# LayerNorm steps of Wo's second wave and of w1 set to new places in a hand-written order

## The chip, the cores and the metric

The kernel runs on one core of a Trainium2 chip. The metric is the device time of one execution in microseconds (us). The engines are TensorE (PE, matmuls), VectorE (DVE), ScalarE (ACT), GpSimd (POOL) and SyncE (SP, which here only issues DMAs). Each engine works through its own queue in the order in which the program issues to it, and waits where an instruction needs a result of another engine or a DMA.

## The reference

An adaptive-LayerNorm block with two parts. `mod = silu(c) @ w_mod` gives six rows `sa, ca, ga, sb, cb, gb`. Then, for x of 2048 tokens by 1024:

```
h = layernorm(x) * (1 + ca) + sa
x = x + ga * A(h)        # segment-recurrent attention, 32 heads; its last product is o @ Wo
h = layernorm(x) * (1 + cb) + sb
x = x + gb * B(h)        # B: gelu(layernorm(h) @ w1), shifted by 1 or 2 tokens in four
                         # column groups, @ w2, + h; then gelu(layernorm(.) @ w3) @ w4, + .
```

What matters here is the way from `o @ Wo` to `@ w1`. For each token: the product is multiplied by `ga`, x is added, a LayerNorm gives `u`, which is modulated by `(1 + cb)` and `sb`, and a second LayerNorm gives `z`. `z`, transposed, is an operand of `@ w1`. Both the sum (`x1`) and the modulated `u` are needed later, so both are written to HBM.

## The kernel before, in words

Tokens are in 16 tiles of 128. Tile 0 holds the first 32 tokens and the last 96; tile t holds tokens 32 + 128(t - 1) and the 127 after it. The part that the change touches is a stretch of 144 units of TensorE, numbered n = 0 to 143, of 8 matmuls of 128x512 each.

Units 0 to 111 are `o @ Wo` in two waves of 56 (`wave(0)`, `wave(1)`, L938 to L1005). A wave covers 1024 tokens (8 tiles) by all 1024 columns, as a 2x2 block product with seven products in place of eight (Strassen's form, Winograd's variant). The products come in the order 1, 2, 5, 6, 3, 7, 4 (`ORDER`), each in two halves of four units. So in wave 1 product 1 is units 56 to 63, 2 is 64 to 71, 5 is 72 to 79, 6 is 80 to 87, 3 is 88 to 95, 7 is 96 to 103 and 4 is 104 to 111. Four PSUM banks ("b") serve products 1, 6, 7 and 4, four others ("d") products 2, and then 5 and 3. Behind a product's second half (`after`, L956) either ScalarE copies a bank (`snap`, L946), or VectorE forms a result: `fin` (L949) adds a copy to the bank (L952) where there is one and multiplies by `ga` (L954). Tiles 8 to 11 get their two column halves after products 2 and 3, tiles 12 to 15 after 7 and 4. VectorE also forms the sums and differences of the operand: `sums` (L992, the operation is L1002) has four for each half, which `sums1[hf][k]` numbers: k = 0 is X (for product 5), 1 is f21 (product 7), 2 is f11 (product 6), 3 is f12 (product 3).

Units 112 to 143 are `@ w1` (`A_units`, L1225): four blocks of 512 tokens, eight units each, with a gelu on ScalarE behind each unit (L1231). They go round eight banks, so unit n needs the gelu of unit n - 8. Block 0 needs tiles 0 to 4 of z transposed, block 1 tiles 4 to 8, block 2 tiles 8 to 12, block 3 tiles 12 to 15 and the rest of tile 0.

Between, each tile t goes through these steps:

- `load_x2` (L1114): x from HBM, a DMA issued by POOL, into one of two buffers.
- `C1_x` (L1138): POOL adds x to the two column halves (L1141), and they are written to HBM (L1145; issued by POOL up to tile 8, by SP from tile 9).
- `ln_stats` (L1122): VectorE takes statistics (two BN_STATS, an aggregation and two small ones, L1125 to L1129), POOL the power and one product (L1131, L1132).
- `C1_u` (L1147): ScalarE normalizes into u (two instructions, L1151), one of three buffers.
- `C1_mod` (L1153): VectorE multiplies and adds two rows (L1155, L1156) and takes statistics of the result (L1125 again), POOL the power and one product.
- `C1_z` (L1160): ScalarE normalizes into z (L1163).
- `C1_out` (L1165): a transposing DMA of z (L1174) and the write of u (L1168), issued by ACT up to tile 8 and by SP from tile 9.

The order is written by hand. `put(n, ...)` hangs functions behind unit n, and in a `manual_schedule` the units are issued with what hangs behind them, so every queue's order follows from the numbers:

```
for n in range(8, 144):
    units[n]()
    for f in at.get(n, []):
        f()
```

Each tile had a start (L1255), and its steps followed it at fixed distances: x at 0, statistics at 2, u at 3, modulation at 6, z at 8, out at 9. Also hung in this stretch: `load_w1` (unit 79), `late_slots` (98: the rest of tile 0's transposes and one write, on ACT's queue), `open_h1` and `load_w2` (111). Loads of w3 that follow the stretch ("ring", L1303) are placed by the scheduler and stand between the last tiles' DMAs on SP's queue.

Of the kernel before, what the change touches and what calls it, by code (L numbers as in the profile page):

```python
# [29 lines left out]
NTT = S // P  # L30
# [30 lines left out]
def kernel(ctx, tc, A_x, A_mem0, A_Wq, A_Wk, A_Wv, A_Wo, A_seg_len, B_x, B_w1, B_w2, B_w3, B_w4, c, w_mod, out,  # L61
# [102 lines left out]
    def p_rows(t):  # L164

        if t == 0:
            return [(slice(0, 32), slice(0, 32)), (slice(32, 128), slice(S - 96, S))]
        return [(slice(0, P), slice(32 + P * (t - 1), 32 + P * t))]

    def first_pass(late_hook):  # L170
# [15 lines left out]
        ves = mpool.tile([P, NTT], F32, name="ves")  # L186
# [748 lines left out]
        x1s = {}  # L935
# [178 lines left out]
        def load_x2(t):  # L1114
            if t < NTT and t not in xts2:
                xts2[t] = tp.tile([P, D], BF16, name="xt2")
                for rows, toks in p_rows(t):
                    nc.gpsimd.dma_start(xts2[t][rows, :], x2[toks, :])
# [3 lines left out]
        def ln_stats(t, halves, rstd):  # L1122
            stt = bsm.tile([P, 2, 6], F32, name="ln_st")
            for i in range(2):
                nc.vector.bn_stats(out=stt[:, i, :], in_=halves[i])  # L1125
            mv = bsm.tile([P, 2], F32, name="ln_mv")
            nc.vector.bn_aggr(out=mv[:], in_=stt[:])
            nc.vector.tensor_scalar(mv[:, 1:2], mv[:, 1:2], EPS, None, ALU.add)
            nc.vector.tensor_scalar(mv[:, 0:1], mv[:, 0:1], -1.0, None, ALU.mult)  # L1129
            nmr = bsm.tile([P, 1], F32, name="ln_nmr")  # L1130
            nc.gpsimd.tensor_tensor(rstd, mv[:, 1:2], mhalf[:], ALU.pow)  # L1131
            nc.gpsimd.tensor_tensor(nmr[:], mv[:, 0:1], rstd, ALU.mult)  # L1132
            ln[t] = nmr[:], rstd

        def halves_of(ap):
            return [ap[:, n * 512:(n + 1) * 512] for n in range(2)]

        def C1_x(t):  # L1138
            for n in range(2):
                cs = slice(n * 512, (n + 1) * 512)  # L1140
                nc.gpsimd.tensor_tensor(x1s[t, n][:], x1s[t, n][:], xts2[t][:, cs], ALU.add)  # L1141
            for n in range(2):
                cs = slice(n * 512, (n + 1) * 512)
                for rows, toks in p_rows(t):
                    (nc.sync if t > 8 else nc.gpsimd).dma_start(x1_d[toks, cs], x1s[t, n][rows, :])  # L1145

        def C1_u(t):  # L1147
            nmr, rstd = ln[t]
            us[t] = tu.tile([P, D], BF16, name="u")
            for n, dst in enumerate(halves_of(us[t][:])):  # L1150
                nc.scalar.activation(dst, x1s[t, n][:], ACT.Identity, bias=nmr, scale=rstd)  # L1151

        def C1_mod(t):  # L1153
            u = us[t]
            nc.vector.tensor_tensor(u[:], u[:], cb1_b[:], ALU.mult)  # L1155
            nc.vector.tensor_tensor(u[:], u[:], sb_b[:], ALU.add)  # L1156
            rstd = bsm.tile([P, 1], F32, name="ln_rstd")
            ln_stats(t, halves_of(u[:]), rstd[:])

        def C1_z(t):  # L1160
            nmr, rstd = ln[t]
            zs[t] = (tz if t else tz0).tile([P, D], BF16, name="z")
            nc.scalar.activation(zs[t][:], us[t][:], ACT.Identity, bias=nmr, scale=rstd)  # L1163

        def C1_out(t):  # L1165
            C1b(t)()
            for rows, toks in p_rows(t):
                (nc.sync if t > 8 else nc.scalar).dma_start(u_d[toks, :], us[t][rows, :])  # L1168
# [7 lines left out]
        def C1b(t):  # L1176
            def f():
                if t == 0:
                    turn_z(t, slice(0, 32), 0)
                elif t == 8:  # L1180
                    for r in (slice(0, 64), slice(64, 96), slice(96, P)):
                        turn_z(t, r, 32 + P * (t - 1) + r.start)
                else:
                    turn_z(t, slice(0, P), 32 + P * (t - 1))
            return f

        def next_a(key, hf=None):
            def f():
                for x in range(2) if hf is None else (hf,):
                    load_a(1, key, x)  # L1190
            return f
# [7 lines left out]
        U1, sums1, _ = wave(1)  # L1199
# [39 lines left out]
        def put(n, *fs):  # L1239
            at.setdefault(n, []).extend(fs)  # L1240
# [6 lines left out]
        put(31, next_a((0, 0)))  # L1247
        put(39, next_a((1, 0)))
        put(47, next_a((1, 1)))
        for n, (hf, k) in {57: (0, 0), 59: (1, 0), 72: (0, 1), 74: (0, 2), 76: (1, 1), 78: (1, 2), 83: (0, 3), 85: (1, 3)}.items():  # L1250
            put(n, sums1[hf][k])
        put(79, load_w1)
        put(98, late_slots)
        put(111, open_h1, load_w2)
        starts = [40, 45, 50, 55, 60, 76, 81, 86, 97, 101, 105, 109, 113, 116, 119, 122]  # L1255
        for t, n in enumerate(starts):
            put(max(n - 9, starts[t - 2] if t > 1 else 0), lambda t=t: load_x2(t))
            put(n, lambda t=t: C1_x(t))
            put(n + 2, lambda t=t: ln_stats(t, [x1s[t, k][:] for k in range(2)], ves[:, t:t + 1]))
            put(n + 3, lambda t=t: C1_u(t))  # L1260
            put(n + 6, lambda t=t: C1_mod(t))
            put(n + 8, lambda t=t: C1_z(t))
            put(n + 9, lambda t=t: C1_out(t))
        put(134, check_b)
        for k in range(KT):
            put(135 + k, lambda k=k: check_a(k))
# [977 lines left out]

    cond_box = []
    first_pass(None if no_fallback else (lambda: cond_box.append(load_flag())))
    if no_fallback:
        return
# [51 lines left out]
```

## Time and profile before

| | us |
|---|---|
| median of 5 runs | 1460.7 |
| lowest, highest | 1455.13, 1481.52 |
| the profiled execution | 1456.59 |
| its span | 1454.8 |
| TensorE busy | 1399.4 (96%) |
| VectorE busy | 980.2 (67%) |
| ScalarE busy | 688.2 (47%) |
| POOL busy | 474.5 (33%) |
| matmuls of `o @ Wo` (L987) | 776.1 to 977.3 |
| matmuls of `@ w1` (L1230) | 977.3 to 1045.1 |

In lines of the timeline the columns are start, length, engine, line, operation, output<-inputs, shapes and count; in square brackets stands how long the engine sat idle before it and what ended that. Consecutive instructions of one kind are merged into one line with their count. In windows, "PEclk" is the share of full speed that TensorE's clock was granted.

### The profile page before, as it was taken

The numbers are of one execution on the slowest core, as the hardware profiler recorded it, in microseconds if no ns is written. First come the engines' busy times: TensorE is split into PE (matmuls) and PEld (weight loads), VectorE is DVE, ScalarE is ACT, GpSimd is POOL, SyncE is SP. The second block draws the span as 40 slices with busy tenths as digits, with TensorE's granted clock in tenths as the row PEclk, the third lists the DMA queues.
The fourth block names the chain that finished last, engine by engine and source line by source line (L and its number), as shares of the span: only waits on it lengthen the run. The fifth ranks groups of instructions, "written<-read, shape, count | busy, mean of one in ns | idle before, by whom it ended". The sixth has DMA issues, their size and how long they took to land.

```text
span 1454.8 us, 24753 instructions
## 1 busy us (share of the span) xinstructions
PE 1399.4 (96%) x9126; PEld 739.6 (51%) x9126; DVE 980.2 (67%) x1995; ACT 688.2 (47%) x1468; POOL 474.5 (33%) x656
## 2 busy tenths in 40 slices
PE   6998999999999999999999999999899999999998
PEld 4675555555555555555555444444343444444443
DVE  6627776777776777777754647887257567666684
ACT  3625556565665656566664013226355650056400
POOL 6120321503222202220001025655224663645525
PEclk9999999999999999999999999999999999999999
DMA  9778978878787776777759999968499783477812
GB/s 327 272 237 201 184 169 201 213 177 205 178 198 195 171 177 172 177 198 181 160 137 305 362 372 296 303 198 255 134 289 244 234 277 107 152 235 250 282 40 79
DMA packets 389237, 310.69 MB, mean 214 GB/s; under 512 B 199658, under 2 KB 336874, under 8 KB 385266
## 3 DMA queue, kind: packets, MB, share of 16 engines
q1 hardware_dynamic: 356576, 244.03, 62.0%
q0 software_dynamic: 13856, 46.16, 9.2%
q10 hardware_dynamic: 18674, 18.83, 4.6%
q8 instruction: 73, 1.20, 0.3%
q14 instruction: 58, 0.48, 0.1%
HBM read 199.38 MB, written 59.02 MB: 178 GB/s over the span
## 4 chain that ended last, share of the span: by engine, by line
PE 73%; DVE 10%; DMA 9%; ACT 3%; issue 3%; POOL 1%; SPq 0%; DVEq 0%; POOLq 0%; ACTq 0%
PE acc L649 26%; PE acc L987 10%; PE bank_b L1509 7%; PE bank_b L1458 6%; PE acc L323 3%; PE bank_d L1458 3%; DMA s<-OTw_d 3%; PE bank_e L1509 2%; PE bank_d L1509 2%; PE acc L333 2%; PE acc L1230 2%; PE acc L1368 2%; PE ps_o L774 2%; PE bank_e L1458 2%; DMA wk<-in_A_Wk_dram 2%
## 5 line engine op out<-in xcount | busy, mean ns | idle before, releaser
L649 PEld LDWEIGHTS <-T 128*128 128x128 f16 x1408 | 129.9, 97 | 122.2 <-issue 6.8
L617 ACT COPY snap<-acc 128x480 f32<-128x480 f32 x264 | 146.0, 565 | 90.8 <-PE acc L649 84.1
L987 PE MATMUL acc<-wstream,s 128*128 128x512 f16 (+1 forms) x864 | 187.3, 379 | 1.2 <-DMA wstream<-in_A_Wo_dram 0.7
L649 PE MATMUL acc<-hs,T 128*128 128x480 f16 x704 | 159.7, 366 | 4.1 <-DVE QT L621 2.0
L649 PE MATMUL acc<-hh,T 128*128 128x480 bf16 (+1 forms) x704 | 162.5, 366 | 0.4 <-DVE KT L621 0.3
L987 PEld LDWEIGHTS <-s 128*128 128x128 f16 (+1 forms) x864 | 84.2, 98 | 103.8 <-DVE s L1002 1.8
L1458 PEld LDWEIGHTS <-ring 128*128 128x128 f16 (+1 forms) x784 | 76.7, 98 | 101.1 <-issue 9.4
L799 POOL DMA_DIRECT2D OTw_d<-OT x32 | 24.8, 774 | 259.7 <-DMA OT<-O 208.7
L761 ACT ACTIVATE E<-ps_s 99x495 bf16<-99x495 f32 (+2 forms) x160 | 88.0, 551 | 40.5 <-PE ps_s L757 40.0
L649 PE MATMUL acc<-hh,wq 128*128 128x480 bf16 x464 | 105.6, 366 | 0.0
L781 DVE TENSOR_TENSOR O<-ps_o,rin_all 99x384 bf16<-99x384 f32 (+1 forms) x192 | 97.3, 510 | 3.9
L1423 ACT COPY snap<-bank_b 128x512 f32<-128x512 f32 x72 | 41.8, 586 | 105.4 <-PE bank_b L1509 58.2
L621 DVE TENSOR_TENSOR KT<-acc,snap 128x480 bf16<-128x480 f32 x116 | 74.4, 654 | 22.5 <-PE acc L649 16.0
L774 PE MATMUL ps_o<-V,E 99*128 99x129 bf16 (+1 forms) x704 | 81.0, 220 | 8.5 <-DVE O L781 2.9
L1509 PEld LDWEIGHTS <-hq 128*128 128x128 bf16 (+1 forms) x560 | 54.7, 98 | 66.2
L763 DVE TENSOR_TENSOR E<-E,maskB 99x495 bf16<-99x495 bf16 (+1 forms) x128 | 53.4, 418 | 47.9 <-ACT E L761 46.2
L1292 DVE TENSOR_TENSOR ring<-ring 128x1024 f16<-128x1024 bf16 (+1 forms) x64 | 78.4, 1244 | 4.3 <-PE bank_b L1509 3.8
L774 PEld LDWEIGHTS <-E 99*128 99x128 bf16 (+1 forms) x704 | 57.0, 98 | 46.0 <-DVE O L781 4.8
L779 ACT ACTIVATE O<-ps_o,rin_all 99x128 bf16<-99x128 f32 x192 | 56.7, 370 | 41.7 <-DVE rin_all L776 41.4
L1509 PE MATMUL bank_b<-ring,hq 128*128 128x512 f16 (+1 forms) x336 | 73.2, 379 | 0.0
L1462 ACT ACTIVATE hq<-join 128x512 bf16<-128x512 f32 x84 | 52.8, 630 | 42.9 <-DVE join L1466 42.9
L621 DVE TENSOR_TENSOR VT<-acc,snap 128x480 bf16<-128x480 f32 x90 | 58.0, 651 | 21.5 <-PE acc L649 15.3
(268 smaller groups left out, 2681.4 us busy)
## 6 DMA issues: line engine op xcount, KB each, us to landing
OTw_d<-OT POOLq DMA_DIRECT2D x32, 512.0 KB, 5.9
wstream<-WoT_d SPq DMA_DIRECT2D x16, 1024.0 KB, 8.8
wstream<-in_B_w_dram SPq DMA_DIRECT2D x28, 512.0 KB, 5.2
ring<-in_B_w_dram SPq DMA_DIRECT2D x28, 512.0 KB, 5.5
ring<-in_B_w_dram SPq DMA_DIRECT2D x8, 1792.0 KB, 10.1
s<-OTw_d SPq DMA_DIRECT2D x13, 1024.0 KB, 8.1
wstream<-in_A_Wo_dram SPq DMA_DIRECT2D x11, 1024.0 KB, 11.5
wq<-in_A_Wq_dram SPq DMA_DIRECT2D x16, 512.0 KB, 5.7
```

What stands on the lines that cost most here:

```text
L617: nc.scalar.copy(t[:], st[q][bank][:, 0:CH])
L621: nc.vector.tensor_tensor(view(d, i), chunks(st[q][bank]), chunks(st[q][s_]), ALU.add)
L649: nc.tensor.matmul(acc[:, 0:CH], lhsT=B[:, k, :], rhs=A[:, k, :], start=(j in (1, 2, 5) and k == 0), stop=(k == 3), skip_group_check=True)
L761: nc.scalar.activation(E[:rows, 0:o], ps[:rows, 0:o], ACT.Exp, scale=DH ** -0.5)
L763: nc.vector.tensor_tensor(E[:rows, 0:o], E[:rows, 0:o], mk[:rows, 0:o], ALU.mult)
L774: nc.tensor.matmul(ps[:, i, :], lhsT=state["e", h, t // 5][:k, c:c + P], rhs=V[:k, t, 0:DH + 1], start=True, stop=True)
L779: nc.scalar.mul(O[:rows, t, :], ps[:rows, i, 0:DH], rin[:, i:i + 1])
L781: nc.vector.tensor_tensor(O[:rows, ts[0]:ts[0] + n, :], ps[:rows, 0:n, 0:DH], rin[:, :, None].to_broadcast([rows, n, DH]), ALU.mult)
L987: nc.tensor.matmul(acc[:], lhsT=A[:, k, i * P:(i + 1) * P], rhs=B[:, k, :], start=(j in (1, 2, 5) and hf == 0 and k == 0), stop=(hf == 1 a ...
L1292: return nc.vector.tensor_tensor(dst, a, b, op)
L1458: nc.tensor.matmul(acc[:], lhsT=B[:, k, q * P:(q + 1) * P], rhs=A[:, k, :], start=(start and k == 0), stop=(k == 3), skip_group_check=True)
L1509: nc.tensor.matmul(acc[:], lhsT=L3[:, k, i * P:(i + 1) * P], rhs=R3[:, k, :], start=(start and k == 0), stop=(k == 13), skip_group_check=True)
```

## The change

The table of starts with fixed distances gives way to two tables, one for the statistics and one for the modulation. x stands two units ahead of the statistics, u one behind them; z follows the modulation by two units (three from tile 8 on), out by three (four). Where several steps hang behind one unit they are sorted: x, load, statistics, u, modulation, z, out. Before they stood in the order of the tiles.

Six of the eight operand sums of wave 1 move as well: f21 from units 72 and 76 to 65 and 66, f11 from 74 and 78 to 72 and 73, f12 from 83 and 85 to 76 and 79.

In units, before and after:

| tile | 3 | 4 | 5 | 6 | 7 | 8 | 9 | 10 | 11 | 12 | 13 | 14 | 15 |
|---|---|---|---|---|---|---|---|---|---|---|---|---|---|
| statistics before | 57 | 62 | 78 | 83 | 88 | 99 | 103 | 107 | 111 | 115 | 118 | 121 | 124 |
| statistics after | 57 | 61 | 63 | 74 | 79 | 95 | 98 | 101 | 104 | 112 | 114 | 117 | 119 |
| modulation before | 61 | 66 | 82 | 87 | 92 | 103 | 107 | 111 | 115 | 119 | 122 | 125 | 128 |
| modulation after | 61 | 66 | 77 | 81 | 85 | 98 | 104 | 107 | 110 | 114 | 117 | 119 | 122 |

Tiles 0 to 2 keep these two places. On SP's queue the scheduler's ring loads move too: four of six stood around the last two tiles' transposes (two ahead of tile 14's, two ahead of tile 15's) and now stand behind them all; two others now stand ahead of tile 13's.

```diff
-        for n, (hf, k) in {57: (0, 0), 59: (1, 0), 72: (0, 1), 74: (0, 2), 76: (1, 1), 78: (1, 2), 83: (0, 3), 85: (1, 3)}.items():
+        for n, (hf, k) in {57: (0, 0), 59: (1, 0), 65: (0, 1), 66: (1, 1), 72: (0, 2), 73: (1, 2), 76: (0, 3), 79: (1, 3)}.items():
             put(n, sums1[hf][k])
...
-        starts = [40, 45, 50, 55, 60, 76, 81, 86, 97, 101, 105, 109, 113, 116, 119, 122]
-        for t, n in enumerate(starts):
-            put(max(n - 9, starts[t - 2] if t > 1 else 0), lambda t=t: load_x2(t))
-            put(n, lambda t=t: C1_x(t))
-            put(n + 2, lambda t=t: ln_stats(t, [x1s[t, k][:] for k in range(2)], ves[:, t:t + 1]))
-            put(n + 3, lambda t=t: C1_u(t))
-            put(n + 6, lambda t=t: C1_mod(t))
-            put(n + 8, lambda t=t: C1_z(t))
-            put(n + 9, lambda t=t: C1_out(t))
+        stat = [42, 47, 52, 57, 61, 63, 74, 79, 95, 98, 101, 104, 112, 114, 117, 119]
+        mod = [46, 51, 56, 61, 66, 77, 81, 85, 98, 104, 107, 110, 114, 117, 119, 122]
+        steps = []
+        for t in range(NTT):
+            late = t > 7
+            xn = stat[t] - 2
+            steps += [(max(xn - 9, stat[t - 2] - 2 if t > 1 else 0), 1.5, lambda t=t: load_x2(t)),
+                      (xn, 1, lambda t=t: C1_x(t)),
+                      (stat[t], 2, lambda t=t: ln_stats(t, [x1s[t, k][:] for k in range(2)], ves[:, t:t + 1])),
+                      (stat[t] + 1, 3, lambda t=t: C1_u(t)),
+                      (mod[t], 4, lambda t=t: C1_mod(t)),
+                      (mod[t] + 2 + late, 5, lambda t=t: C1_z(t)),
+                      (mod[t] + 3 + late, 6, lambda t=t: C1_out(t))]
+        for n, _, f in sorted(steps, key=lambda x: x[:2]):
+            put(n, f)
```

## The prediction

> **What bounds the kernel now.** I read the page's busy table first, then TensorE's waits and its timeline around the changed stage, then the other engines' timelines there.
>
> ```profile
> PE 1399.4 (96%) x9126; PEld 739.6 (51%) x9126; DVE 980.2 (67%) x1995; ACT 688.2 (47%) x1468; POOL 474.5 (33%) x656
> ```
>
> TensorE is the bound: only 1454.8 - 1399.4 = 55.4 us of the span are idle on it. A schedule edit can gain only what it waits for in this stage. Its waits from 880 to 1045 us (columns: total, times, longest):
>
> ```profile
> PE acc L1230 <- DMA s<-z: 5.4, 1, 5.4
> PE acc L1230 <- ACT u L1151: 3.0, 1, 3.0
> ```
>
> No wait in Wo's second wave, two in w1. TensorE's timeline shows where:
>
> ```profile
> 977.28 27.79 PE L1230 MATMUL acc<-zA,s 128*128 128x512 bf16 x128
> 1008.07 15.66 PE L1230 MATMUL acc<-s,s 128*128 128x512 bf16 x64 [3.00 <-ACT u L1151]
> 1029.16 16.02 PE L1230 MATMUL acc<-s,s 128*128 128x512 bf16 x64 [5.43 <-DMA s<-z]
> ```
>
> 128 matmuls of w1 take 27.79 us, so 64 should take 13.9. The two later blocks took 15.66 and 16.02, which is 1.8 and 2.1 us more. The windows of L1230 show why (length, PE busy, PEld busy, granted clock, DMA share, GB/s):
>
> ```profile
> 1009.00:1013.00 4.00, 4.00 (x13) 1.41 (x12) 0.57 0.38 133
> 1029.00:1033.00 4.00, 3.84 (x10) 1.36 (x11) 0.50 0.05 13
> 1037.00:1041.00 4.00, 4.00 (x20) 1.85 (x19) 1.00 0.00 0
> ```
>
> After each idle stretch the clock is half for about 3.5 us. The two waits therefore cost 3.0 + 5.4 + 1.8 + 2.1 = 12.3 us. That is the most that can be gained here (0.84%).
>
> Next VectorE and POOL ahead of unit 72 (units are numbered as in the schedule; one is 8 matmuls, 1.73 us; unit 111 ends at 977.28, so unit 72 starts at 908.1). VectorE:
>
> ```profile
> 891.24 2.28 DVE L1002 TENSOR_TENSOR s<-s,s 128x4096 f16<-128x4096 bf16 x1
> 895.78 1.19 DVE L1155 TENSOR_TENSOR u<-u,cb_b 128x1024 bf16<-128x1024 bf16 x1 [2.26 <-ACT u L1151]
> ...
> 903.62 0.69 DVE L1155 TENSOR_TENSOR u<-u,cb_b 128x1024 bf16<-128x1024 bf16 x1 [2.42 <-ACT u L1151]
> ...
> 906.76 0.68 DVE L952 TENSOR_TENSOR snap<-acc,snap 128x512 f32<-128x512 f32 x1
> ```
>
> The last line reads the bank that unit 72 writes again (product 5 takes the four accumulator banks of product 2). It ends at 907.45, 0.6 us before it is due.
>
> POOL, and VectorE beside it (two views):
>
> ```profile
> 894.15 2.27 POOL L1141 TENSOR_TENSOR x<-x,xt 128x512 f32<-128x512 f32 x2
> 896.37 1.14 POOL L1145 DMA_DIRECT2D x_d<-x x2
> ...
> 952.21 2.27 POOL L1141 TENSOR_TENSOR x<-x,xt 128x512 f32<-128x512 f32 x2
> ```
> ```profile
> 952.25 2.79 DVE L954 TENSOR_TENSOR x<-snap,ga_b 128x512 f32<-128x512 f32 x1
> ```
>
> The multiplication with two operands in SBUF, 0.69 us elsewhere, took 2.79: it ended 0.56 us after POOL's pair of additions. Where VectorE comes second it waits for the whole pair.
>
> **What the Trainium skill says.** "SBUF — State Buffer", section "SBUF: two separate sides", has the port pair of VectorE and GpSimd as an exclusive lock for the whole instruction, for VectorE operations with two SBUF inputs too; the 2.79 us agrees. "TensorE: Matmul & The Clock Gate", Part 1, halves the clock after an idle window of about 3.4 us and restores it after as much work; here 3.0 us of idling were enough, so the trace decides. The same page ("Architectural detail") calls ScalarE's and VectorE's queues strict FIFO, on which the arguments on order rest; every stretch of the timelines shows it.
>
> **The change part by part.** Write S(t) for a tile's statistics (1.7 us on VectorE), M(t) for its modulation with second statistics (3.15 us free of POOL, 3.65 when it starts inside an addition), fin for a product's result (1.35 with a snapshot, 0.65 without), x(t) for POOL's addition of x (2.27).
>
> *Nothing is added or removed*: the same instructions move. What counts is the order in each queue.
>
> *Units 57 to 71.* Between the second sum (ends 893.5) and the first fin at 906.76 VectorE now does M3, S4, M4 with 2.26 and 2.42 us of waiting. After, it does S4, M3, S5, two sums (moved from units 72 and 76 to 65 and 66), M4, fin. S4 needs x(4), which ends at 896.42 as before, so S4 ends at 897.6. M3 takes 3.65: 901.25. S5: 902.95. Two sums of 2.28: 907.5. M4: 910.65. The L952: 911.35. Unit 72 waits from 908.1 to 911.4: 3.3 us. But x(5) is moved directly behind x(4) and its write, so it starts at 897.5, in a tie with M3. The pair holds VectorE off until 899.8, which makes M3 about 1.6 longer: wait 4.9. I take the middle, 4.1, and 1.8 for the clock (the 3.0 us wait cost that): **5.9 us lost**; ends 3.3 (clock kept) and 6.9. The u of M4 doesn't decide: S4's power stands behind x(5) and its write on POOL (900.95), u(4) ends near 903.3, M4 starts at 907.5.
>
> *Units 92 to 111* (times without that delay, which shifts TensorE and what depends on it alike). From the last fin of product 3 (950.9) VectorE does S8 1.7; S9, which ends 4.15 later because x(9) stands behind S8's power on POOL (0.8 + 2.27 + 1.1); M8 3.65; four fins 5.6; S10 and S11 3.4; two waits for the pairs x(10), x(11), about 1.6 each; M9 and M10 6.6; three fins 2.0. Sum: 981.3. The fins of product 7 come after S10 now, so unit 106 may wait about 0.7.
>
> *Last tiles.* M11 waits 1.1 for x(12)'s pair and ends near 986; one fin, S12 and S13: 990.8. S12's power stands behind x(13) and an xt load on POOL (991.2), u(12) takes 1.5, M12 ends at E = 995.9. Behind its power POOL does x(14) and x(15) together: E + 5.3. M13 waits for that pair: E + 8.3. S15: E + 10.1. Its power (up to 1 us, against M14) and u(15): E + 12.6. Now ScalarE, in order: z(13) stands behind u(15), and the gelu of unit 121 behind z(13): E + 14.5 = 1010.4. Unit 129 takes that gelu's bank and is due at 977.28 + 17 x 1.737 = 1006.8: **a wait of about 3.6 us**. Tile 12's transpose, behind the writes of x(14) and x(15) on SP, is issued at E + 6.7 = 1002.6; transposes of this stage land after 2.4 to 8.4 us, so block 2 (due 1005.1) waits up to 6 in the same place, not on top. With the clock 5.4, plus the 0.7: **6.1 us lost** in place of 12.3. Tile 15's transpose is issued near 1016 and the ring loads that stood before the last two transposes on SP now stand after them (one but for tile 13); with 4 to 6.5 us it lands by 1022.5, before block 3 is due (1005.1 + 5.4 + 13.9 = 1024.4). Cover there: 2 us.
>
> *Other moves cost nothing.* u ahead of the previous z on ScalarE in wave 1 (z is used some 90 units later), f11 and f12 earlier (f11 ready about 918 and 921, due at 922 and 929; f12 about 925 and 930, due at 936 and 943; units 83 to 85 get that time back), loads of xt and writes of x_d earlier (covered by four ring buffers of weights, 20 us ahead). Behind w1 everything hangs on TensorE and moves with it.
>
> **Sum**: -12.3 + 5.9 + 6.1 = -0.3 us. On the profiled execution, 1456.6: 1456.3; on the median of the runs, 1460.7, which is 4.1 above it: **1460.4**.
>
> **Rivals.**
> 1. *The last tiles keep up.* For: S and M run back to back, and u(t) is ready a tile early. Against: POOL's order above. Only the wave's wait and 0.7 are left: -12.3 + 6.6 = -5.7, 1455.0.
> 2. *The wave doesn't wait long enough to lose clock.* For: only a 1.6 us tie and a 0.6 us margin separate them. Against: the sum gives at least 3.3. -12.3 + 2.4 + 6.1 = -3.8; with rival 1 too it is -9.2: 1451.5 to 1457.
> 3. *Slower: SP and POOL become w1's bound.* Tile 12's transpose waits for x(15) on POOL through the writes ahead of it. If it lands after 8.4 us, block 2 waits 6 + 1.8, and block 3 follows with 2 + 0 to 1.8 as u(15) waits for u_d(12), queued behind the transpose (u has three buffers). With 6.9 in the wave, 6.9 + 0.7 + 7.8 + 3 = 18.4: +6.1, 1466.8. It decides from a landing of about 6.5 us on (a wait over 3.9, which with its clock, 5.9 and 0.7 passes 12.3). For: landings of 6.5 to 8.4 stand in this stage. Against: the w2 load that made them lies earlier.
> 4. *It does nothing*: excluded, since each queue's order changes.
>
> **How the numbers follow.** Forecast 0.38, within 4 us; rival 1 0.20; rival 2 0.14, half of it together with rival 1; rival 3 0.16; steps that I haven't seen 0.12, as likely to help as to harm. Below 1453.4 (0.5%, 7.3 us, about what a measurement of this kernel can tell from no change) lie two fifths of rival 1 (0.08), the half of rival 2 that comes with rival 1 and a little more (0.09), and 0.07 of the rest: 0.24. Above 1468.0 lie half of rival 3 (0.08), 0.04 of the forecast, 0.05 of the unseen: 0.17. Same: 0.59. The range, 1450 to 1468, leaves out the full double success and the worst of rival 3; the forecast's own is 1456 to 1465.
>
> **What would show it.** TensorE's waits list a stall at unit 72 (product 5's first matmul) on VectorE's snap, 3 to 5 us, with half clock behind it; a POOL pair x(5) lies over M3. In w1 the wait for the transpose before the last block is gone, and a wait of 2 to 4 us stands at the third block, on a gelu or tile 12's transpose. Wrong: no wait in the wave (VectorE kept the port), or M12 done well before E plus the shift.

## The result, and the profile after

The changed kernel is slower than forecast, and its times spread. Its median is 1473.3 us over 26 runs, from 1451.8 to 1485.4; the kernel before, timed beside it, has 1459.2 over 47 runs, 43 of them below 1463.2. Of the changed kernel's 26 only seven are below 1463. The ratio is 1.0023 with the interval 1.0005 to 1.0042; this ratio leaves out executions more than 1.5% above the fastest of the same kernel, which here are many, so the median over all runs stands beside each ratio below. The forecast was 1460.4 with a range of 1450 to 1468: the median lies outside.

The profiled execution of the changed kernel is one of the shortest: 1451.75 us (before: 1456.59), span 1450.0. Its busy table:

```profile
PE 1397.8 (96%) x9126; PEld 740.3 (51%) x9126; DVE 979.4 (68%) x1995; ACT 688.1 (47%) x1468; POOL 487.2 (34%) x656
```

The work is the same. What differs is what TensorE waits for, here from Wo's first matmul to the end of w1 (its waits: total, times, longest):

```profile
PE acc L987 <- DVE snap L952: 4.6, 2, 4.4
...
PE acc L987 <- DMA wstream<-in_A_Wo_dram: 1.3, 2, 1.0
PE acc L1230 <- ACT s L1231: 1.1, 1, 1.1
```

The two waits of w1 (5.4 on a transpose, 3.0 on u) are gone. In their place stand 4.4 us at unit 72, as foretold, and 1.1 on a gelu. TensorE's timeline, with the start and length of each stretch and the idle time before it:

```profile
909.28 37.48 PE L987 MATMUL acc<-wstream,s 128*128 128x512 f16 x160 [4.40 <-DVE snap L952]
...
972.24 10.52 PE L987 MATMUL acc<-wstream,s 128*128 128x512 f16 x48 [0.17 <-DVE snap L952]
982.59 28.06 PE L1230 MATMUL acc<-zA,s 128*128 128x512 bf16 x128
...
1013.50 26.06 PE L1230 MATMUL acc<-s,s 128*128 128x512 bf16 x120 [1.12 <-ACT s L1231]
```

The 160 matmuls behind the stall took 37.48 us where the kernel before needs 34.6 (0.2163 us each), so 2.9 us went to the clock. The windows of L987 show it (length, PE busy, PEld busy, granted clock, DMA share, GB/s):

```profile
909.00:913.00 4.00, 3.72 (x9) 1.28 (x9) 0.50 1.17 372
913.00:917.00 4.00, 4.00 (x15) 1.62 (x14) 0.76 1.00 174
```

Added up, this trace has lost 7.3 (stall and clock), 1.0 on a late load of weights and 1.3 on the two last waits shown, and gained 12.3: 2.7 us. It is 4.8 us shorter, but most of that lies ahead of the stage, where the change moves nothing. The kernel before starts Wo's first matmul at 776.1, and this trace at 772.1:

```profile
L987 PE MATMUL acc<-pre_w,pre_o x32: 376/378/382, 772.1 to 783.5; 128*128 128x512 bf16 x32
```

From that matmul to the end of w1 it took 267.4 us, the kernel before 269.0. So in a short execution the change gains 1.6 us: Wo takes 9.3 longer and w1 10.9 less. In the 19 traces of this document the same matmul starts between 772.0 and 780.7, whatever the kernel, so single traces are best compared stage by stage. The open question was what makes most of its executions 15 to 30 us longer.

### The profile page after: what moved, and what is told of

Same layout as the page of the kernel before. It is cut to its first block, busy times and chain, and to the rows that moved or that the text cites. A ratio compares the mean times of both kernels' runs of the same rounds, so it can differ in the third digit from the quotient of the medians.

```text
span 1450.0 us, 24752 instructions
## 1 busy us (share of the span) xinstructions
PE 1397.8 (96%) x9126; PEld 740.3 (51%) x9126; DVE 979.4 (68%) x1995; ACT 688.1 (47%) x1468; POOL 487.2 (34%) x656
## 4 chain that ended last, share of the span: by engine, by line
PE 68%; DVE 12%; DMA 9%; ACT 4%; issue 3%; POOL 3%; ACTq 1%; SPq 1%; DVEq 0%; POOLq 0%
PE acc L649 27%; PE bank_b L1515 7%; PE bank_b L1464 6%; PE bank_d L1464 3%; DMA s<-OTw_d 3%; PE acc L987 3%; PE acc L323 3%; PE bank_d L1515 3%; PE bank_e L1515 3%; PE acc L333 2%; PE ps_o L774 2%; PE acc L1374 2%; DVE ln_st L1125 2%; DMA wk<-in_A_Wk_dram 2%; PE acc L1230 2%
## 5 line engine op out<-in xcount | busy, mean ns | idle before, releaser
L987 PE MATMUL acc<-wstream,s 128*128 128x512 f16 (+1 forms) x864 | 190.7, 383 | 7.3 <-DVE snap L952 4.6
L987 PEld LDWEIGHTS <-s 128*128 128x128 f16 (+1 forms) x864 | 84.9, 99 | 112.5 <-issue 11.7
L621 DVE TENSOR_TENSOR KT<-acc,snap 128x480 bf16<-128x480 f32 x116 | 74.6, 655 | 22.5 <-PE acc L649 15.7
L1298 DVE TENSOR_TENSOR ring<-ring 128x1024 f16<-128x1024 bf16 (+1 forms) x64 | 82.1, 1303 | 5.5 <-PE bank_b L1515 5.1
## 6 DMA issues: line engine op xcount, KB each, us to landing
wstream<-WoT_d SPq DMA_DIRECT2D x16, 1024.0 KB, 14.8
```

The lines of the kernel that those rows point to most:

```text
L621: nc.vector.tensor_tensor(view(d, i), chunks(st[q][bank]), chunks(st[q][s_]), ALU.add)
L987: nc.tensor.matmul(acc[:], lhsT=A[:, k, i * P:(i + 1) * P], rhs=B[:, k, :], start=(j in (1, 2, 5) and hf == 0 and k == 0), stop=(hf == 1 a ...
L1298: return nc.vector.tensor_tensor(dst, a, b, op)
```

## The experiments

**Theory A**: the fixed waits just shown are all that counts. **Theory B**: in many executions something more is lost in the wave; the candidates were the low clock behind the stall, transfers in the wave, and the last tiles. Of each edit, only the lines that differ are shown.

### The changed kernel again, and its three parts

The first run is the changed kernel unedited.

> The changed kernel once more, for a second trace and more times. Its first trace (1451.8 us, 1.3 us under the fastest trace-independent time of the kernel before) gains 4.8 us, while the median of its times is some 14 us longer and its times lie between 1452 and 1485. Theory A (fixed waits: only what the schedule makes late counts): times within some 6 us of 1452. Theory B (in many executions something more is lost): times again between 1452 and 1485, with the median 5 to 15 us above the kernel before; if a long one is traced, it lists a wait or a stretch of low granted clock that the first trace hasn't.

Measured: median 1473.2 over 6 runs (1466.2 to 1488.0), ratio 1.0106 (1.0049 to 1.0163). Theory B. The traced execution took 1467.65 us. TensorE's waits in the whole of it, and the two stretches of its timeline that follow the longest:

```profile
PE acc L987 <- DMA wstream<-WoT_d: 11.6, 3, 9.4
...
PE acc L987 <- DVE snap L952: 4.4, 1, 4.4
```
```profile
968.02 7.07 PE L987 MATMUL acc<-wstream,s 128*128 128x512 f16 x32 [1.86 <-DMA wstream<-WoT_d]
984.46 15.96 PE L987 MATMUL acc<-wstream,s 128*128 128x512 f16 x64 [9.37 <-DMA wstream<-WoT_d]
```

The stall at unit 72 is the same in both traces. What is new is late weights: 11.2 us in two waits (the third, 0.4, lies in the first wave), with half clock behind the second (64 matmuls in 15.96 us in place of 13.9). The spans differ by 15.9; 6.1 of that lie ahead of Wo's first matmul (778.2 against 772.1), and Wo itself takes 11.6 longer.

The next run has the changed steps, with the sums where they were:

```diff
-        for n, (hf, k) in {57: (0, 0), 59: (1, 0), 65: (0, 1), 66: (1, 1), 72: (0, 2), 73: (1, 2), 76: (0, 3), 79: (1, 3)}.items():
+        for n, (hf, k) in {57: (0, 0), 59: (1, 0), 72: (0, 1), 74: (0, 2), 76: (1, 1), 78: (1, 2), 83: (0, 3), 85: (1, 3)}.items():
```

> The changed steps of all tiles, but the sums of products 5 and 6 at the units where the kernel before has them (f21 at 72 and 76, f11 at 74 and 78, f12 at 83 and 85). Theory A: two sums of 2.28 us no longer stand ahead of M4, so unit 72 waits at most 0.5 us where the changed kernel waits 4.4 with 2 to 3 of clock behind it; the trace is 5 to 7 us shorter than the changed kernel's (1445 to 1447). Spread: if the long executions come from the stall and the low clock that it starts, the times now lie within 6 us of each other and the ratio to before is 0.991 to 0.994; if they come from transfers in the wave or from the last tiles, the spread of some 30 us stays and the ratio is near 1.000.

Measured: median 1469.0 over 22 runs (1456.4 to 1481.6), ratio 1.0046 (1.0021 to 1.0072). The stall at unit 72 is gone (0.74 us are left in its trace), but the spread stays. So the stall and its clock are not what makes executions long. The traced one (1474.7) again waits for weights, and for a sum that is late for another reason:

```profile
PE acc L987 <- DMA wstream<-WoT_d: 7.1, 2, 4.7
PE acc L987 <- DMA wstream<-in_A_Wo_dram: 5.1, 1, 5.1
PE acc L987 <- DVE s L1002: 5.1, 1, 5.1
```

The sum stands behind S6 on VectorE, which waited 10.9 us for x(6), and POOL had waited 17.7 us for the load of xt that x(6) needs.

Then the tiles apart. The wave alone has the new sums, the new tables for tiles 0 to 7 and the old starts and distances for tiles 8 to 15 (`old_steps` holds the seven `put` of the kernel before):

```diff
-        for t in range(NTT):
+        for t in range(8):
...
+        for t in range(8, NTT):
+            old_steps(t)
```

> The changed steps for tiles 0 to 7 and the changed sums, tiles 8 to 15 as in the kernel before. Theory A: the stall at unit 72 (4.4 us and 2 to 3 of clock) on top of the two waits of w1 (12.3 us): 6 to 7 us longer than before, ratio 1.004 to 1.005, w1's two waits back. Spread: wide (30 us) if it comes from the stall or from transfers of the wave; narrow (6 us) if it comes from the last tiles.

Measured: median 1478.6 over 21 runs (1463.0 to 1490.3), ratio 1.0093 (1.0065 to 1.0122), none below 1462. Wide, so the cause lies in the wave. In its trace w1's two waits are back beside the stall:

```profile
PE acc L1230 <- DMA s<-z: 10.6, 2, 8.1
PE acc L987 <- DVE snap L952: 4.0, 1, 4.0
```

The late tiles alone are the mirror image (old starts and sums for tiles 0 to 7, new tables for 8 to 15):

```diff
-        for t in range(NTT):
+        for t in range(8):
+            old_steps(t)
+        for t in range(8, NTT):
```

> Tiles 0 to 7 and the sums as in the kernel before, the changed steps for tiles 8 to 15. Theory A: no wait in the wave, w1 with one wait of 1 to 4 us in place of 12.3: 8 to 11 us shorter than before, ratio 0.992 to 0.995. Spread: narrow if it comes from the wave, wide (30 us) and a ratio near 1.000 if it comes from the last tiles.

Measured: median 1453.0 over 22 runs (1446.5 to 1475.9, 20 of them below 1462), ratio 0.9943 (0.9921 to 0.9965). The late tiles bring 7.2 us against the 1460.2 of the kernel before, timed beside it. So the wave's part of the change costs 1473.2 - 1453.0 = 20 us, of which the prediction had 5.9.

### What is late in the wave

The view of DMAs from 925 to 1000 us gives, for each queue, packets, bytes and the time that they took as a share of 16 engines, then issues with the median time to landing. q10 carries ScalarE's DMAs: the transposes and the writes of u. The kernel before:

```profile
q10 hardware_dynamic: 5840, 2.59, 18.7%
...
wstream<-WoT_d SPq DMA_DIRECT2D x4, 1024.0 KB, 6.3
```

The changed kernel in the 1467.65 us execution:

```profile
q10 hardware_dynamic: 5840, 2.59, 48.3%
...
wstream<-WoT_d SPq DMA_DIRECT2D x4, 1024.0 KB, 17.7
...
u_d<-u ACTq DMA_DIRECT2D x4, 256.0 KB, 27.1
```

The same 5840 packets with the same 2.59 MB took 2.6 times as long (the times of packets overlap, as shares above 1 show). The 17.7 us are a median of two landings, 12.9 and 22.5; the trace doesn't tell those of the other two loads. In this trace's windows the engines are full while little moves:

```profile
960.00:970.00 10.00, 8.14 (x39) 3.61 (x38) 4.24 (x12) 0.00 (x0) 3.69 (x6) 1.00 1.26 72
```

72 GB/s at a share of 1.26; from 860 to 880 us the same trace moves 376 GB/s at 1.02.

The last two loads of weights are also issued late. SP's waits in the same stretch, in the kernel before and in this execution:

```profile
SPq L932 <- PE acc L987: 24.0, 4, 6.5
```
```profile
SPq L932 <- DMA u_d<-u: 16.3, 1, 16.3
```

In the kernel before SP issues each load when TensorE has done with a buffer, every 6.9 us. Here it waits for tile 5's write of u, which the change issues earlier, and issues the next one at 962.16, 16.7 us after the one before it. TensorE's wait of 9.4 us is for this load and ends 22.3 us after its issue. In the trace the write and the load tell of their landing by the same semaphore, which would explain the wait. No run took away this wait alone, so its share of the loss isn't shown.

The short execution has the same wait of SP (16.3 us) and the same median of 17.7 us, and in it one issue of a transpose held ScalarE for 14.8 us:

```profile
937.01 14.81 ACTq L1174 DMA_TRANSPOSE zA<-z  x1
```

So the slow transfers are no feature of long executions alone. There the load behind SP's wait, issued at 956.57, was in place when its matmuls were due at 968.45, and TensorE didn't wait for it.

**Theory C**: a transpose beside the weights slows both. **Theory D**: it is only the bytes. To tell them apart, the transposes of tiles 1 to 7 become plain DMAs of the same bytes in the same pieces (z then stays untransposed):

```diff
+            if 0 < t < 8:
+                nc.scalar.dma_start(zTs[0][:, :, tok:tok + n],
+                                    zs[t][rows, :].rearrange("p (k c) -> p k c", c=P))
+                return
             (nc.sync if t > 8 else nc.scalar).dma_start_transpose(...)
```

> The changed kernel with the DMA transposes of tiles 1 to 7 replaced by plain DMAs of the same bytes in pieces of 256 bytes, from the same queue to the same place (z then isn't transposed, so that the result differs). In the long executions of the first job, weights of the wave land after up to 22 us and stretches of some 10 us move 40 to 150 GB/s where 250 to 400 is usual. Theory C (a transpose that shares the DMA engines with the wave's weights slows both): these stretches are gone, weights land within 13 us, TensorE's waits for weights in the wave are under 2 us together, the stall at unit 72 stays at 3 to 4.5 us, and the times are 1449 to 1457. Theory D (only the number of bytes counts): as the changed kernel, 1466 to 1488 with a median near 1473.

Measured: median 1452.1 over 20 runs, all between 1449.1 and 1457.2; ratio 0.9953 (0.9935 to 0.9971). Theory D falls and C stands. The same view of the trace:

```profile
q10 hardware_dynamic: 5792, 2.59, 12.7%
...
wstream<-WoT_d SPq DMA_DIRECT2D x4, 1024.0 KB, 9.7
```

Its TensorE waits 4.4 us at unit 72 and at most 0.7 for any weights. SP still waits for the write of u, but 7.7 us in place of 16.3. Three runs put single steps of tiles 5 to 7 back. The first moves z and what follows it:

```diff
+            zn = {5: 84, 6: 89, 7: 94}.get(t, mod[t] + 2 + late)
-                      (mod[t] + 2 + late, 5, lambda t=t: C1_z(t)),
-                      (mod[t] + 3 + late, 6, lambda t=t: C1_out(t))]
+                      (zn, 5, lambda t=t: C1_z(t)),
+                      (zn + 1, 6, lambda t=t: C1_out(t))]
```

> The changed kernel with z of tiles 5, 6 and 7, their transposes and their writes of u back at units 84, 89 and 94 (79, 83 and 87 in the changed kernel). If these transposes, moved into the stretch with the most weights, make the wave's loads late, the median falls from 1473 to 1455 to 1462; if it is the loads and writes of x, it stays within 4 us of 1473.

Measured: median 1455.5 over 20 runs (1448.6 to 1483.5), ratio 0.9985 (0.9961 to 1.0008). Most of the loss is gone, and in its trace SP waits for no write of u before a load of weights. But 8 of 20 are still above 1462, the longest at 1483.5.

The second moves the writes of x, which become a step of their own:

```diff
         def C1_x(t):
...
+            if not 4 < t < 8:
+                C1_xd(t)
+
+        def C1_xd(t):
...
+        steps += [(n, 1.2, lambda t=t: C1_xd(t)) for t, n in {5: 76, 6: 81, 7: 86}.items()]
```

> The changed kernel with the writes of x of tiles 5, 6 and 7 back at units 76, 81 and 86 (61, 72 and 77 in the changed kernel); the additions of x stay ahead. If these writes fill the DMA engines in the wave, the median falls to 1455 to 1462; if the transposes or the loads do, it stays within 4 us of 1473.

Measured: 1475.5 over only 4 runs (1455.2 to 1481.9), ratio 1.0126 (1.0065 to 1.0188). As far as four runs tell, the writes of x are not it.

The third puts everything of these tiles back and keeps sums and late tiles as changed:

```diff
-        stat = [42, 47, 52, 57, 61, 63, 74, 79, 95, 98, 101, 104, 112, 114, 117, 119]
-        mod = [46, 51, 56, 61, 66, 77, 81, 85, 98, 104, 107, 110, 114, 117, 119, 122]
+        stat = [42, 47, 52, 57, 61, 78, 83, 88, 95, 98, 101, 104, 112, 114, 117, 119]
+        mod = [46, 51, 56, 61, 66, 82, 87, 92, 98, 104, 107, 110, 114, 117, 119, 122]
```

> The changed kernel with all steps of tiles 5, 6 and 7 back at the units of the kernel before; sums, tiles 0 to 4 and tiles 8 to 15 as changed. M4 then has no statistics of tile 5 ahead of it, only the two sums: unit 72 waits 1 to 2.5 us in place of 4.4. If the long executions come from the early steps of tiles 5 to 7, the times are as with the late tiles alone plus that wait: median 1453 to 1458, within 10 us of each other save a few. If the sums alone suffice to make weights late, the median is above 1465.

Measured: median 1451.7 over 20 runs, 1445.8 to 1461.0, ratio 0.9941 (0.9924 to 0.9959). This is the version to keep: it beats both kernels. Unit 72 waits 0.56 us, less than expected, and the clock holds. So the moved sums alone cost next to nothing; the stall needs the early x and statistics of tile 5 as well.

### Which transposes

The kernel before with plain DMAs (the edit of the first of these, in the kernel before):

> The kernel before with the transposes of tiles 1 to 7 replaced by plain DMAs of the same bytes (z isn't transposed, the result differs). Theory C says that a transpose which shares the DMA engines with weights slows both; in the kernel before this is seldom long enough to reach TensorE, so the ratio to before is 0.998 to 1.000, w1's two waits stay (12 us with their clock), and the few times above 1464 are gone. If plain copies made the kernel faster for a reason of their own, by the 20 us that they took off the changed kernel, the median would be near 1440.

Measured: 1459.6 over 12 runs (1454.5 to 1464.4), ratio 0.9996 (0.9977 to 1.0014); the two waits of w1 stand (2.8 and 5.8 us). Plain DMAs give nothing of their own, so the 21 us between the changed kernel with and without transposes are a price that they have in the changed order alone. One run was 0.35 us above the bound of 1464.

The changed steps with the sums back and plain DMAs (both edits above together):

> The changed steps with the old places of the sums, and the transposes of tiles 1 to 7 replaced by plain DMAs (z isn't transposed). Beside the changed sums with plain DMAs (1452.1) this has the price of the stall at unit 72 alone: 4.4 us and 2.4 to 2.9 of clock. Theory A and C together: no wait over 1 us in the wave, median 1445 to 1447, all within 8 us. If the sums have no part in it, 1451 to 1453.

Measured: 1448.9 over 4 runs (1447.1 to 1452.7), ratio 0.9932 (0.9906 to 0.9957). With the sums back unit 72 waits 1.1 us and the clock holds. But the gain over the same with moved sums is 3.1 us, not the 5 to 7 expected; with four runs, how much of the stall is got back later is left open.

Then plain DMAs for some of the tiles, in the changed kernel: `4 < t < 8`, those that the change moves, and `0 < t < 5`, those that it doesn't.

> The changed kernel with plain DMAs in place of the transposes of tiles 5, 6 and 7 alone, those that the change moves (z of these tiles isn't transposed). If only these meet the weights, the times are as with all seven replaced: median 1451 to 1454, all under 1459. If the transposes of tiles 1 to 4, which the change leaves in place, collapse as well because loads and additions of x now lie beside them, a part of the times stays above 1462 and the median is 1455 or more.

Measured: 1453.2 over 9 runs, all between 1449.1 and 1458.1, ratio 0.9963 (0.9941 to 0.9985).

> The changed kernel with plain DMAs in place of the transposes of tiles 1 to 4 alone, which the change leaves in place (z of these tiles isn't transposed). If only the moved transposes of tiles 5 to 7 count, the median stays at 1466 to 1476; if those of tiles 1 to 4 count, it falls below 1460.

Measured: 1477.4 over 13 runs (1460.1 to 1489.3), ratio 1.0088 (1.0059 to 1.0116). The pair is clear: without the transposes of tiles 5, 6 and 7 the loss is gone, without those of tiles 1 to 4 it isn't. The traced execution of the second (1480.6 us) shows it at its worst; TensorE's waits, and ScalarE's queue (start, length of the issue):

```profile
PE acc L987 <- DMA wstream<-WoT_d: 24.6, 3, 19.3
```
```profile
938.28 1.34 ACTq L1177 DMA_TRANSPOSE zA<-z  x1
...
942.62 10.26 ACTq L1177 DMA_TRANSPOSE zA<-z  x1
...
956.29 18.64 ACTq L1177 DMA_TRANSPOSE zA<-z  x1
...
979.23 1.52 ACT L1151 ACTIVATE u<-x,ln_nmr,ves 128x512 bf16<-128x512 f32 x2 [22.96 <-issue]
```

The issue of the second takes 10 us and that of the third 19. ScalarE computes nothing from 956 to 979, and the u that stands behind in its queue waits 23 us. In the kernel before the same three stand apart and each takes 1.25:

```profile
937.73 1.25 ACTq L1174 DMA_TRANSPOSE zA<-z  x1
...
945.57 1.25 ACTq L1174 DMA_TRANSPOSE zA<-z  x1
...
952.97 1.25 ACTq L1174 DMA_TRANSPOSE zA<-z  x1
```

### Why there and not in the kernel before

The gap was the next theory: 7.4 to 7.8 us between these issues before, 4.3 between the first two now. One run takes the middle transpose out (`t == 6` alone plain):

> The changed kernel with a plain DMA in place of the transpose of tile 6 alone (z of this tile isn't transposed): 18 us then lie between the transposes of tiles 5 and 7. If a transpose that is issued while another is still in flight beside weights is what collapses, the long times go: median 1451 to 1455, all under 1460. If any transpose of these tiles at its new place collapses, a part stays above 1462 and the median is 1456 or more.

Measured: 1459.7 over 20 runs (1452.1 to 1469.0), ratio 1.0001 (0.9977 to 1.0026). Most of the loss goes, but not all.

Another brings two together in the kernel before:

```diff
-            put(n + 8, lambda t=t: C1_z(t))
-            put(n + 9, lambda t=t: C1_out(t))
+            put(89 if t == 5 else n + 8, lambda t=t: C1_z(t))
+            put(89 if t == 5 else n + 9, lambda t=t: C1_out(t))
```

> The kernel before, with z of tile 5, its transpose and its write of u moved behind unit 89, directly ahead of those of tile 6; nothing else is moved. If two transposes close together collapse, the times spread as those of the changed kernel do: median 1464 to 1475, highest above 1478. If the place among the weights counts and not the gap, it stays within 3 us of the kernel before.

Measured: 1457.4 over 12 runs (1455.1 to 1463.3), ratio 1.0002 (0.9985 to 1.0020). Its trace has the two 3.8 us apart (942.65 and 946.41), each issued in under 1.7 us. There a small gap alone costs nothing; the theory falls.

One run sets the modulation of tiles 5 to 7 back to units 82, 87 and 92, and with it z and out, and leaves x, statistics and u early:

> The changed kernel with the modulation of tiles 5, 6 and 7 back at units 82, 87 and 92, and with it z and out; x, statistics and u of these tiles stay early, and so does the stall at unit 72. Waiting for the modulation sets the transposes 7 us or more apart again. If the gap counts: median 1450 to 1454, all under 1460. If loads and additions of x that lie early count beside it, a part stays above 1462, as with z alone at its old place.

Measured: 1459.6 over 20 runs (1451.0 to 1481.2), ratio 1.0001 (0.9980 to 1.0023). Of the 7.9 us above the version with all steps of these tiles back, some 6.8 may be the stall at unit 72 (an estimate: 4.44 us in this trace against 0.56 in the other, and 2.9 of clock, as in the first trace). But 4 of 20 are above 1466, and in its trace q10 is slow although the transposes are at their old units:

```profile
q10 hardware_dynamic: 7799, 3.52, 44.6%
```

TensorE doesn't wait for weights in the wave there, but a second time for a snap of VectorE, 6.6 us at unit 104. The next run shows by which way.

Two last runs asked for the second cause. The first moves the writes of x back too (this edit and that of the writes together):

> The changed kernel with modulation, z and out of tiles 5 to 7 at the old units, and their writes of x back at units 76, 81 and 86 as well; only the loads and additions of x, the statistics and u are early. If the early writes of x are the second cause, the long times go: median 1450 to 1454, all under 1461. If the loads are, it stays at 1457 to 1462 with times above 1466.

Measured: 1461.2 over 20 runs (1453.9 to 1468.6), ratio 1.0002 (0.9985 to 1.0020): no gain. Its trace (1467.3 us) has no wait for weights either. Here the issue of a plain write of u holds ScalarE; VectorE's M8 waits for the u behind it, and TensorE, at unit 104, for the snap that stands behind M8 (ScalarE, VectorE and TensorE; line numbers of this kernel, four above those used so far for these steps):

```profile
962.42 14.45 ACTq L1172 DMA_DIRECT2D u_d<-u  x1
...
976.98 1.52 ACT L1155 ACTIVATE u<-x,ln_nmr,ves 128x512 bf16<-128x512 f32 x2 [19.84 <-DMA x_d<-x]
```
```profile
978.53 0.69 DVE L1159 TENSOR_TENSOR u<-u,cb_b 128x1024 bf16<-128x1024 bf16 x1 [13.45 <-ACT u L1155]
```
```profile
982.41 16.58 PE L987 MATMUL acc<-wstream,s 128*128 128x512 f16 x64 [13.59 <-DVE snap L952]
```

The changed table of the late tiles has put M8 ahead of that snap (unit 98, before 103). So slow transfers reach TensorE by two ways at least, through weights and through ScalarE's queue.

The second has the early writes of x again, and plain DMAs for tiles 1 to 4:

> The changed kernel with modulation, z and out of tiles 5 to 7 at the old units, and plain DMAs in place of the transposes of tiles 1 to 4 (z of these isn't transposed). If the early x makes these four collapse and the rest follows from that, the long times go: median 1450 to 1454, all under 1461. If the transposes of tiles 5 to 7 still collapse by themselves, it stays at 1457 to 1462 with times above 1466.

Measured: 1458.3 over 12 runs (1452.6 to 1467.6), ratio 0.9983 (0.9959 to 1.0007). In its trace the queue is quick again (16.3% for 2.59 MB). That fits early x making the transposes of tiles 1 to 4 slow, but the medians of these three runs lie within 3 us of each other, each has one trace, and this one is of a short execution (1453.2).

**What is settled and what isn't.** Shown: the long executions of the changed kernel need the transposes of tiles 5 to 7. With these as plain DMAs none is left (1453.2), with those of tiles 1 to 4 all but one are above 1466 (1477.4). Shown too: most of the loss comes with the new place of z, transposes and writes of u (1455.5 with these back), and the long executions that are left go when every step of these tiles is back (1451.7, none above 1461). The stall at unit 72 doesn't make them, nor does the gap alone in the kernel before, nor, by four runs, do the writes of x. Argued from single traces: the ways by which slow transfers reach TensorE (weights issued late behind a write of u and landing late, ScalarE held at an issue, a late load of xt). Open: what makes a transpose slow at the new place, why it reaches TensorE in some executions and not in others, and what early x adds. That it needs the loads of weights beside it is argued from the traces, where the slow stretches hold both; no run took the weights away.

## Why the prediction was wrong, point by point

- **"Other moves cost nothing" is the step that failed.** It priced the loads of xt and the writes of x, and called both covered by four buffers of weights, 20 us ahead. It did not list the transposes and writes of u of tiles 5 to 7, which the change issues 5 to 7 units earlier, and it had no term for what one transfer does to another. The runs put about 20 us in that place: 1473.2 against 1453.2 with the three transposes replaced. The 20 us of cover hold only while loads are issued every 6.9 us and land soon. The load that TensorE waited for longest was issued 9.8 us late in the long trace and 13.3 in the worst, and the wait ended 22.3 and 33.2 us after its issue. Nor were the loads of xt covered everywhere: with the sums back, a late one made a sum late and TensorE wait 5.1 us. The rivals held no such case; it fell among the unseen steps, to which 0.12 was given.
- **Unit 72: right in place and kind.** The prediction had 3.3 to 4.9 us with 4.1 in the middle. Of ten traces with the sums and tile 5's x, writes of x and statistics as changed, eight have 4.35 to 4.44, one 3.97 and one 5.70. The detail differs between executions. In the first trace x(5) waited for its load, so M3 ran free; u(4) then came late, because POOL's power stood behind the two sums. The line is VectorE's `L1155` of M4:

```profile
899.28 4.48 DVE L1002 TENSOR_TENSOR s<-s,s 128x4096 f16<-128x4096 bf16 x2
905.40 0.69 DVE L1155 TENSOR_TENSOR u<-u,cb_b 128x1024 bf16<-128x1024 bf16 x1 [1.63 <-ACT u L1151]
```

  and POOL's two small operations beside it, which take 0.55 and 0.19 us elsewhere:

```profile
899.69 2.30 POOL L1131 TENSOR_TENSOR ves<-ln_mv,mhalf 128x1 f32<-128x1 f32 x1
902.06 1.75 POOL L1132 TENSOR_TENSOR ln_nmr<-ln_mv,ves 128x1 f32<-128x1 f32 x1
```

  "The u of M4 doesn't decide" was therefore wrong in this execution: the port pair that the prediction cites held POOL off as well as VectorE. In the long trace M3's first operation is the one that takes 2.80 us, as foretold. Two ways lead to the same 4.4.
- **The clock behind it: 1.8 foretold, 2.9 measured.** The price came from one wait of 3.0 us. Behind the same stall of 4.35 to 4.40 us three other traces lost some 1.7, 2.3 and 2.7 (320 matmuls in 70.94, 71.46 and 71.93 us, where 69.2 are needed), so one wait doesn't give a price.
- **w1: 12.3 us gained, as said; 6.1 given back, where 1.3 was measured.** The gelu that unit 129 needs is the right one. But M12 ended 2.3 us earlier than the sum had it: E was 995.9, plus the 5.3 by which unit 112 started later than before, against 998.9 in the trace. The waits for POOL's pairs that were added before it did not all come. ScalarE's lines behind it, u(15), z(13) and the gelus that wait for both:

```profile
1010.32 1.52 ACT L1151 ACTIVATE u<-x,ln_nmr,ves 128x512 bf16<-128x512 f32 x2 [2.31 <-POOL ln_nmr L1132]
1011.74 1.23 ACT L1163 ACTIVATE z<-u,ln_nmr,ln_rstd 128x1024 bf16<-128x1024 bf16 x1
1012.88 1.06 ACT L1231 ACTIVATE s<-acc 128x512 bf16<-128x512 f32 x2
```

  The order is the forecast's, some 2.4 us sooner, so the wait is 1.1 in place of 3.6, and no clock was lost behind it. Rival 1 came true within w1: it took 57.0 us in place of 67.9. But unit 106, to which the prediction gave 0.7 us, waited 1.65 in each of four traces with the late tiles as changed (the late tiles alone among them), and by the medians the late tiles alone are worth 7.2 us. That lies nearer to the forecast's 6.2 than to the rival's 11.6.
- **Rival 3**, slower through SP and POOL in w1, did not happen: tile 12's transpose was never waited for.

The sum with measured terms: -12.3 + 7.3 + 1.0 + 1.3 = -2.7 for a short execution (measured from Wo's first matmul to the end of w1: -1.6), and about 20 more at the median. That the forecast of -0.3 is near the short execution is in part luck: Wo cost 9.3 us where 6.6 were forecast, and w1 gave 10.9 where 6.9 were.

## What to carry to other kernels

When a step is moved into a stretch where the DMA engines are full, list every transfer that it issues and ask what each does to the others and who waits for it (the queue that it is issued from, and other queues that wait for its landing), not only how many bytes it adds: here transposes of 256 KB went with loads of 1 MB that were issued and landed late. A wider spread of the times is a result too. The trace of a short execution may hold the slow transfers and still not the waits for them; trace a long one, then replace the suspected transfer by a plain one of the same bytes. Compare single traces by stage, since a part of their difference can lie where nothing was changed. Of a change with several parts, keep the part that gains: here the late tiles (1453.0 alone, 1451.7 with the moved sums, which the runs don't tell apart), without the early steps of tiles 5 to 7.

## What the runs showed of the hardware

- The Trainium skill ("Advanced Engine Details and Errata", section "X-Bar Transpose (TRN2)") calls transposing DMAs as fast as regular ones. Beside full loads of weights they are not: over the same 75 us, q10's 2.59 MB took 12.7% of 16 engines with plain DMAs in place of those of tiles 1 to 7, 18.7% in the kernel before, and 48.3% in a long execution of the changed kernel, where 10 us moved 72 GB/s. The measurement decides for this case.
- When a DMA is held up at its issue, the engine that issues it is held up too: 18.6 us for one transpose, with a u behind it after 23 us of idling, and 14.45 us for a plain write of u on the same queue.
- What a stall of TensorE costs beside itself isn't a smooth function of its length. After 1.7 us (w1, late tiles alone) the clock held: 120 matmuls in 26.06 us, 0.217 each. Between 2.4 and 3.1 us it went both ways: 2.45 us in the kernel before with tile 5 next to 6 was followed by a block of 64 matmuls (63 in the records) in 15.49, 1.6 too many, and 3.06 us in the run with the writes of x put back by 256 in 55.41, none too many. In this stage the traces have half clock in pieces of 3.4 us and whole multiples of it: about the stall of 4.4 us 6.8 in the first two traces and 3.4 in the worst, and 20.5 about the wait of 19.3.
